# Multiplying all columns of a scale vector before the first q matmul, and loading them ahead of the q weights

## The chip, the cores and the metric

One core of a Trainium2 chip. The metric is device time in microseconds (us) of one execution. PE is TensorE, PEld its weight load, DVE VectorE, ACT ScalarE, SP the engine whose queue issues the loads, POOL GpSimd. PSUM is the memory that matmuls write to; copying a result out of it is called its evacuation.

## The reference, cut to what matters

A transformer block with adaptive layer norm: 2048 tokens, width 1024, linear attention, then a gated feed-forward layer. What matters here is the first modulation:

```
mod = silu(c) @ w_mod                       # six vectors of 1024: sa, ca, ga, sb, cb, gb
h = layernorm(x) * (1 + ca) + sa            # ca: the first scale vector, sa: the first shift vector
q, k, v = split(h @ wqkv)
```

## The kernel before: the parts that matter

All loads go through one queue, in program order. `WCA` holds the part of `w_mod` for `ca`, in two halves of 512 columns (1 MB each). `WQK[:, i]` holds the q weights for input slice i (128 of the 1024 inputs; 0.25 MB each).

```
for st in range(4): load x tile st          # 4 x 0.25 MB
ca_load(0)                                  # columns 0..3 (blocks of 128) of the scale vector
wq_load(0, 2)                               # q weights, slices 0 and 1
ca_load(1)                                  # columns 4..7
wq_load(2, 2); wq_load(4, 2); sa_load(1) ...
```

A column block of the scale vector is eight matmuls with one output column each, accumulated in PSUM. DVE then adds 1:

```
def mod_sc(w, c0, ms):
    for m in ms:
        for kt in range(NDT):               # 8
            P.pe("matmul", out=PS[:, 0, c0 + m:c0 + m + 1], lhsT=w[:, kt, m * 128:(m + 1) * 128],
                 rhs=SILUC[:, kt:kt + 1], start=mod_first[0], stop=(kt == NDT - 1), ...)
def fin_ca(m, n):
    P.dve("tensor_scalar", out=MODCOL[:, 0, m:m + n], in0=PS[:, 0, 8 + m:8 + m + n], scalar1=1.0, ...)
```

The front and the first q phase, in program order (each engine works in order; cut):

```
warm(13)                                    # fillers: 128x512 matmuls on zeros
... DVE, ACT: layer norm of tiles 0..3
tile_transposes(0); warm(5); tile_transposes(1)
ln1_xn(2); ln1_xn(3)                        # DVE: normalize tiles 2 and 3
mod_sc(WCA, 8, range(2)); fin_ca(0, 2)      # columns 0,1
tile_transposes(2, 3)
h0_first(0), h0_first(1)                    # DVE: slice of h = (1 + ca) * transposed tiles
# q phase
for nt in range(4): q_part(nt, qb[nt], (0,))
mod_sc(WCA, 8, range(2, 4)); fin_ca(2, 2)   # columns 2,3
h0_first(2), h0_first(3)
... 10 more q matmuls on slices 0 and 1
mod_sc(WCA, 8, range(4, 8)); fin_ca(4, 4)   # columns 4..7
... 14 q matmuls on slices 2 and 3, 8 on slice 4 and 5
mod_sc(WSA, 0, range(6, 8))                 # the first one-column matmuls on the SHIFT columns: "the marker"
```

The start of that last line is called the marker below. Between the first q matmul on slice 2 and the marker there are always the same 22 q matmuls, in every version, so the marker tells when the part that the change touches was over.

## Time and profile before

| | |
|---|---|
| time, median of 3 | 831.89 us (831.71 to 832.13) |
| span of the profiled execution | 829.7 us |
| PE busy | 99% of it |
| marker | 20.76 us |

The page, its part on busy time and its part on the chain that ended last:

```profile
PE 819.3 (99%) x4005; PEld 378.6 (46%) x4083; DVE 311.0 (37%) x665; ACT 196.3 (24%) x335; POOL 40.7 (5%) x58
...
PE 96%; DVE 2%; issue 1%; DMA 0%; ACT 0%; POOL 0%; DVEq 0%; ACTq 0%
```

PE bounds the kernel, and it runs nearly without a gap.

The front on PE's weight loads, from the timeline of the kernel before (start us, length us, group, count, and in brackets the idle time before it and what ended it):

```profile
7.20 0.45 PEld L176 LDWEIGHTS ps<-ident,xres 128*128 128x128 bf16 x8 [0.39 <-DVE xres L176]
7.60 0.80 PEld L176 LDWEIGHTS ps<-e,ident 128*128 128x128 bf16 x5
9.27 0.45 PEld L176 LDWEIGHTS ps<-ident,xres 128*128 128x128 bf16 x8 [0.87 <-ACT xres L176]
9.96 0.46 PEld L176 LDWEIGHTS ps<-siluc,wca 128*128 128x128 bf16 x16 [0.23 <-DMA wca<-in_w_mod_dram]
10.35 0.10 PEld L176 LDWEIGHTS ps<-ident,xres 128*128 128x128 bf16 x1
10.70 0.84 PEld L176 LDWEIGHTS ps<-ident,xres 128*128 128x128 bf16 x15 [0.26 <-DVE xres L176]
11.76 0.56 PEld L176 LDWEIGHTS ps<-ht,wqk 128*128 128x128 bf16 x4 [0.22 <-issue]
12.44 0.67 PEld L176 LDWEIGHTS ps<-siluc,wca 128*128 128x128 bf16 x16
13.03 1.84 PEld L176 LDWEIGHTS ps<-ht,wqk 128*128 128x128 bf16 x10
15.00 1.06 PEld L176 LDWEIGHTS ps<-siluc,wca 128*128 128x128 bf16 x32
15.99 0.55 PEld L176 LDWEIGHTS ps<-ht,wqk 128*128 128x128 bf16 x4
```

Transposes read `xres`, fillers `e`, scale columns `siluc,wca`, q matmuls `ht,wqk`. The first q weights are loaded at 11.76 us. Before 11.76 there are holes. Just one is ended by a load of the scale columns (0.23 us, until 9.96). After it there is none.

What held the first q matmul back is shown by the chain of waits:

```profile
9.29 0.79 POOL rstd L176
10.08 0.03 issue
10.10 0.56 DVE xres L176
10.66 0.05 issue
10.71 1.01 PE ps L176 x15
```

It is the normalization of tile 3 (`xres`, 10.10 to 10.66) and then its transposes.

The loads of the two scale halves, issue and time to landing, from the DMA view of the two stretches in which they are issued (columns: count, KB, us to landing; issued at 2.65 and 4.00 us):

```profile
wca<-in_w_mod_dram SPq DMA_DIRECT2D x1, 1024.0 KB, 7.3
...
wca<-in_w_mod_dram SPq DMA_DIRECT2D x1, 1024.0 KB, 10.3
```

So the first half lands at 2.65 + 7.3 = 9.95 us and the second at 4.00 + 10.3 = 14.3 us. PE uses the second at 15.00: its load is hidden behind q matmuls.

### The profile page before, as it was taken

To read this page: it belongs to the slowest core of one execution; us is meant where nothing else is said; L and a number is where in the kernel's file an instruction comes from. 1 tells how busy PE (TensorE), PEld (TensorE's weight loads), DVE (VectorE), ACT (ScalarE), POOL (GpSimd) and SP (SyncE) were. 2 spreads that over 40 slices of the span, in tenths; PEclk is the share of its full clock that TensorE was granted. 3 is DMA by queue.
4 is the path that set the end of the run, shared out by engine and by line. 5 is a ranking of instruction groups with operands and counts; after the bars stand their busy time and mean duration, and the time that the engine had idled before them with its cause. 6 is when DMAs were issued, how large, how long until landed. Compare 5 with 4: busy or idle time off the path is not lost.

```text
span 829.7 us, 9938 instructions
## 1 busy us (share of the span) xinstructions
PE 819.3 (99%) x4005; PEld 378.6 (46%) x4083; DVE 311.0 (37%) x665; ACT 196.3 (24%) x335; POOL 40.7 (5%) x58
## 2 busy tenths in 40 slices
PE   8999999999999999999999999999999999999998
PEld 4544444454444444444444444444444444444444
DVE  5797986756955521121221112122111111111111
ACT  3757641323232111111111101111110111111011
POOL 1010000000130000030000003000000300000000
DMA  9969656928297995700455571045557004553000
GB/s 321 289 151 231 148 156 172 202 102 304 56 248 233 283 264 153 197 25 13 123 152 152 152 188 34 13 125 152 156 150 192 26 16 125 152 154 88 0 26 26
DMA packets 199247, 119.29 MB, mean 144 GB/s; under 512 B 57881, under 2 KB 182945, under 8 KB 199201
## 3 DMA queue, kind: packets, MB, share of 16 engines
q1 hardware_dynamic: 199184, 118.65, 52.7%
q8 instruction: 32, 0.52, 0.3%
q14 instruction: 15, 0.11, 0.0%
q10 hardware_dynamic: 16, 0.00, 0.0%
HBM read 100.67 MB, written 4.33 MB: 127 GB/s over the span
## 4 chain that ended last, share of the span: by engine, by line
PE 96%; DVE 2%; issue 1%; DMA 0%; ACT 0%; POOL 0%; DVEq 0%; ACTq 0%
PE ps L176 96%; DVE acc L176 1%; DVE stats L176 0%; DMA xres<-in_A_x_dram 0%; DVE pkt L176 0%; DVE e L176 0%; DVE xres L176 0%; DVE pqt L176 0%; POOL rstd L176 0%; DVE mv L176 0%; ACT mw L176 0%; ACT e L176 0%; DVE ve L176 0%; DVE ut L176 0%; DVE ht L176 0%
## 5 line engine op out<-in xcount | busy, mean ns | idle before, releaser
L176 PE MATMUL ps<-h2t,guu 128*128 128x512 bf16 x879 | 210.3, 379 | 0.9
L176 PE MATMUL ps<-h2t,gug 128*128 128x512 bf16 x878 | 209.9, 379 | 0.9
L176 DVE TENSOR_TENSOR at<-sg,ps 128x512 bf16<-128x512 bf16 x112 | 77.0, 687 | 284.8 <-PE ps L176 274.9
L176 ACT ACTIVATE sg<-ps 128x512 bf16<-128x512 f32 x112 | 66.9, 597 | 309.7 <-PE ps L176 298.3
L176 PEld LDWEIGHTS ps<-h2t,guu 128*128 128x128 bf16 x896 | 87.7, 98 | 105.7
L176 PEld LDWEIGHTS ps<-h2t,gug 128*128 128x128 bf16 x896 | 87.6, 98 | 105.5
L176 PE MATMUL ps<-wd_a,at 128*128 128x512 bf16 (+2 forms) x518 | 113.0, 372 | 0.5
L176 PE MATMUL ps<-ht,wqk 128*128 128x512 bf16 x499 | 110.5, 379 | 1.0 <-DVE ht L176 0.3
L176 PE MATMUL ps<-wd_b,at 128*128 128x512 bf16 (+2 forms) x388 | 85.3, 372 | 0.4
L176 PEld LDWEIGHTS ps<-wd_a,at 128*128 128x128 bf16 x528 | 51.0, 98 | 59.8
L176 DVE TENSOR_TENSOR ut<-att,gb_b 128x512 bf16<-128x512 bf16 (+1 forms) x32 | 14.1, 440 | 167.0 <-ACT att L176 167.0
L176 PEld LDWEIGHTS ps<-ht,wqk 128*128 128x128 bf16 x512 | 49.4, 98 | 58.6 <-issue 0.2
L176 ACT ACTIVATE att<-ps 128x512 bf16<-128x512 f32 (+1 forms) x32 | 17.4, 591 | 182.1 <-PE ps L176 182.1
L176 PEld LDWEIGHTS ps<-wd_b,at 128*128 128x128 bf16 x396 | 38.3, 98 | 44.7
L176 PE MATMUL ps<-pk,xres 128*128 128x512 bf16 x250 | 56.0, 379 | 0.4 <-issue 0.2
L176 PE MATMUL ps<-mw,pqt 128*128 128x512 bf16 x250 | 55.7, 379 | 0.3
L176 POOL TENSOR_SCALAR h2t<-h2t,modcol 128x512 bf16<-128x512 bf16 x32 | 26.4, 843 | 383.2 <-DMA h2t<-xn 383.2
L176 ACT ACTIVATE e<-ps 128x512 bf16<-128x512 f32 x56 | 33.2, 604 | 31.7 <-PE ps L176 20.7
L176 PEld LDWEIGHTS ps<-mw,pqt 128*128 128x128 bf16 x256 | 24.9, 98 | 29.9 <-DVE xres L176 0.4
L176 PEld LDWEIGHTS ps<-pk,xres 128*128 128x128 bf16 x256 | 24.8, 98 | 30.1 <-DVE g L176 0.4
L176 ACT ACTIVATE junk<-xres 128x1024 bf16<-128x1024 bf16 x24 | 25.4, 1058 | 35.5 <-DVE xres L176 35.2
L176 DVE SCALAR_TENSOR_TENSOR xres<-ps,xres 128x512 bf16<-128x512 f32 x32 | 21.5, 688 | 12.2 <-PE ps L176 12.0
(102 smaller groups left out, 339.4 us busy)
## 6 DMA issues: line engine op xcount, KB each, us to landing
gug<-in_B_w_gate_dram SPq DMA_DIRECT2D x56, 512.0 KB, 4.0
guu<-in_B_w_up_dram SPq DMA_DIRECT2D x56, 512.0 KB, 5.3
xres<-in_A_x_dram SPq DMA_DIRECT2D x20, 256.0 KB, 7.8
rb<-recip_den SPq DMA_DIRECT2D x8, 512.0 KB, 11.5
stgx<-in_w_mod_dram SPq DMA_DIRECT2D x2, 2048.0 KB, 8.0
wd_a<-in_B_w_down_dram SPq DMA_DIRECT2D x4, 1024.0 KB, 7.9
out_dram<-xres SPq DMA_DIRECT2D x31, 128.0 KB, 1.7
xres<-in_A_x_dram SPq DMA_DIRECT2D x3, 1024.0 KB, 14.1
```

What stands on the lines that cost most here:

```text
L176: return getattr(e, method)(**kw)
```

## The change

Its intent: no one-column matmuls between the first q matmuls. All columns are to be multiplied where PE has holes and runs fillers anyway, and both scale halves are loaded ahead of the q weights so that they come in time. The change also splits the load of q slices 0 and 1 in two and moves two slices of h from DVE to ACT.

```
         ca_load(0)
-        wq_load(0, 2)
         ca_load(1)
+        wq_load(0)
+        wq_load(1)
         wq_load(2, 2)
...
         tile_transposes(0)
-        warm(5, bank=3)
+        warm(3, bank=3)
+        mod_sc(WCA, 8, range(4))
         s3_[0]()
         ln1_xn_act(1)
         tile_transposes(1)
...
         ln1_xn(2)
+        fin_ca(0, 4)
         ln1_xn(3)
-        mod_sc(WCA, 8, range(2))
-        fin_ca(0, 2)
-        tile_transposes(2, 3)
+        tile_transposes(2)
+        warm(2, bank=3)
+        tile_transposes(3)
+        mod_sc(WCA, 8, range(4, 8))
         h0_first(0, "dve")
         h0_first(1, "dve")
+        h0_first(2, "act")
+        h0_first(3, "act")
+        fin_ca(4, 4)
...
-            for nt in range(4):
-                q_part(nt, qb[nt], (0,))
-            mod_sc(WCA, 8, range(2, 4))
-            fin_ca(2, 2)
-            for dt in (2, 3):
-                h0_first(dt, "dve")
-            for nts, dts in (((4, 5), (0,)), (range(6), (1,)), ((6,), (0, 1))):
+            for nts, dts in ((range(4), (0,)), (range(4), (1,)), ((6, 4, 5), (0, 1))):
                 for nt in nts:
                     q_part(nt, qb[nt], dts)
-            mod_sc(WCA, 8, range(4, 8))
-            fin_ca(4, 4)
```

## The prediction

> **What bounds the kernel now.** The page gives PE 99% busy of 829.7 us; the chain that ended last is 96% PE. From the first q matmul (about 11.8 us; timeline) PE runs almost without a gap, so a microsecond won or lost before the second half of the first q phase passes through to the end.
>
> The first 30 us are also DMA-bound: the slices show 350 to 380 GB/s. Landings (DMA view, issue plus time to landing): first half of the scale columns 2.65 + 7.3 = 9.95 us (PE's weight load waits for it, 9.73 to 9.96); q weights 0,1 at 11.3; second half 4.00 + 10.3 = 14.3; q weights 2,3 at 15.7. About 1.5 us lie between the queue having moved a transfer's bytes and its landing. The Trainium skill, "DMA: Bandwidth & Descriptors", section "Anatomy of one DMA", puts a fixed part of about 2 us down mostly to the write receipt; the trace agrees in kind, with 1.5.
>
> **What the change does.** It takes 48 one-column matmuls (16 at 12.65, 32 at 15.21 us; 0.41 + 0.85 us of PE) out of the q phase and puts all 64 before it, where PE has holes (0.38 us at 8.9, 0.23 at 9.73, about 0.3 at 10.4) and fillers (0.22 us each, now 3 + 2 for 5). Bytes are unchanged; the second scale half overtakes q weights 0 and 1.
>
> **What it costs**, estimated from these durations, PE being in order:
> - The first 32 one-column matmuls wait for the landing, still 9.95 us (nothing ahead of it changes), and end at 10.8; PE idles from 8.5. The transposes of tile 1, ready at 9.2, now stand behind them: to 11.25.
> - DVE's normalization of tile 3, now behind the first evacuation, ends near 11.65, not 10.65. Transposes of 2, two fillers, transposes of 3: to about 12.5.
> - The second half lands 0.5 MB earlier: about 12.85. Its 32 matmuls run to 13.7. q weight 0 lands about 13.5, q weight 1 about 14.25: just in time.
> - First q matmul at 13.7 instead of 11.8. The 14 q matmuls on slices 0 and 1, now uninterrupted, take 14 x 0.221 = 3.1 us: to 16.8. Before, those on slices 2,3 begin at 16.23.
>
> So this part gets 1.3 us shorter but begins 1.9 us later: a loss of about 0.55 us. PE waits for no later load, so nothing gives it back. The intent would pay only if the scale columns landed by about 8.5 and 11.8 us; and the q matmuls that hid the second half's load now stand behind it.
>
> **Prediction.** 831.89 + 0.55 = 832.4 us, range 831.8 to 833.2. Faster by over 2%: 0.005; within 2%: 0.99; slower by over 2%: 0.005.
>
> **What would show it.** PE waits about 1.4 us for the first scale load, until 9.95, and again for the second, until 12.85; first q matmul near 13.7, none of one column among the first 14; slices 2,3 begin near 16.8; everything later shifted by the same 0.5 us.
>
> **What would make it wrong.** (1) The second half landing well before 12.8: then equal or slightly faster. (2) The clock gate: the Trainium skill, "TensorE: Matmul & The Clock Gate", section "What's actually happening", says that an idle window of about 3.4 us brings the half clock back. Here matmuls start 0.43 us apart until about 5.8 us, then 0.22. The changed front has holes of 1.4 and 0.4 us among small matmuls; should it fall back, the first q matmuls would be 0.43 us apart and the loss 1 to 3 us. I give this 10%. (3) Slack later, in the stretch at 82 to 95 us where DVE leads the chain, that swallows the shift: then no change.

## More of the kernel before

Every execution has a mean granted TensorE clock in its record (1.0 is full).

The program issues one weight load for each matmul, so 4005 matmul records against 4083 weight loads say that 78 matmul records are missing: where an exact start matters, read the weight loads.

## The result, and the profile after

| | before | after |
|---|---|---|
| median of 6 (same rounds) | 831.80 us | 832.05 us |
| lowest to highest | 831.57 to 832.81 | 831.74 to 832.58 |
| span of the profiled execution | 829.7 | 830.1 |
| first q weight load | 11.76 | 13.39 |
| marker | 20.76 | 21.18 |

Ratio 1.0002, 95% interval 0.9989 to 1.0014: the same. (A ratio is the mean time of one kernel's fast runs over that of the other's in the same rounds, so it is not quite the ratio of the medians.) All executions were fast ones, none of them over 1.5% above the fastest of its kernel.

The chain of waits of the changed kernel, in place of the one through tile 3:

```profile
2.65 0.43 SPq L176
3.08 0.04 issue
3.12 9.43 DMA wca<-in_w_mod_dram
12.55 0.05 issue
12.60 87.41 PE ps L176 x531
```

The first q matmul now hangs on the load of the second scale half, from its issue at 3.12 to its landing at 12.55 us. The front on PE's weight loads:

```profile
7.77 0.69 PEld L176 LDWEIGHTS ps<-ident,xres 128*128 128x128 bf16 x8 [0.28 <-issue]
8.43 0.37 PEld L176 LDWEIGHTS ps<-e,ident 128*128 128x128 bf16 x3
9.62 0.86 PEld L176 LDWEIGHTS ps<-siluc,wca 128*128 128x128 bf16 x32 [0.83 <-DMA wca<-in_w_mod_dram]
10.41 0.90 PEld L176 LDWEIGHTS ps<-ident,xres 128*128 128x128 bf16 x16
11.27 0.15 PEld L176 LDWEIGHTS ps<-e,ident 128*128 128x128 bf16 x2
11.54 0.65 PEld L176 LDWEIGHTS ps<-ident,xres 128*128 128x128 bf16 x8
12.60 0.87 PEld L176 LDWEIGHTS ps<-siluc,wca 128*128 128x128 bf16 x32 [0.41 <-DMA wca<-in_w_mod_dram]
13.39 2.92 PEld L176 LDWEIGHTS ps<-ht,wqk 128*128 128x128 bf16 x15
```

There are two waits for scale columns instead of one, and the first q weights are loaded at 13.39, 1.63 us later. In return the q matmuls run uninterrupted: those on slice 2 begin at about 13.39 + 14 x 0.2156 = 16.41 us, against 15.99 before (0.2156 us is the pace of the 36 q matmuls from 13.42 to the marker at 21.18). The first 14 q matmuls and what stood among them took 4.23 us before and 3.02 after. So 1.63 us later and 1.21 us shorter: 0.42 us lost between these two executions, and the marker and the span show the same 0.4. How much of it is the change comes under e1 and e2.

The time to landing of the two halves, issued at 2.65 and 3.12 us:

```profile
wca<-in_w_mod_dram SPq DMA_DIRECT2D x1, 1024.0 KB, 6.9
...
wca<-in_w_mod_dram SPq DMA_DIRECT2D x1, 1024.0 KB, 9.4
```

In this execution the first half landed at 9.55 us, 0.4 earlier than in the profile of before, although nothing ahead of it in the queue had changed. This spread between executions is the noise that the experiments had to cope with.

### The profile page after: what moved, and what is told of

The parts are those of the page before. It is cut to its first block, busy times and chain, and to the rows that moved or that the text cites. A ratio compares the mean times of both kernels' runs of the same rounds, so it can differ in the third digit from the quotient of the medians.

```text
span 830.1 us, 10017 instructions
## 1 busy us (share of the span) xinstructions
PE 824.2 (99%) x4083; PEld 379.0 (46%) x4083; DVE 310.3 (37%) x662; ACT 197.4 (24%) x337; POOL 40.5 (5%) x58
## 4 chain that ended last, share of the span: by engine, by line
PE 98%; DMA 1%; SPq 0%; ACT 0%; DVE 0%; issue 0%
PE ps L176 98%; DMA wca<-in_w_mod_dram 1%; SPq L176 0%; ACT mw L176 0%; DVE ut L176 0%; DVE xres L176 0%
```

## The experiments

Theory A: PE works in order, so one-column matmuls that stand ahead of the q matmuls hand them the landing time of the scale columns; the gain (48 one-column matmuls out of the q phase) is real but smaller than the delay. Rivals: B, there is no loss, the profiles differ only by when the clock opened, and the order is of little weight; C, a later stretch swallows the shift. D, formed on the way: holes in the front can let the clock gate fall back.

A summary first. "First landing" is the first scale half by the DMA view, "first q" the first q weight load; all from the profiles.

| kernel | first landing | first q | marker | span | span less marker |
|---|---|---|---|---|---|
| before | 9.95 | 11.76 | 20.76 | 829.7 | 808.9 |
| e1 before again | 10.05 | 12.02 | 21.02 | 829.9 | 808.9 |
| after | 9.55 | 13.39 | 21.18 | 830.1 | 808.9 |
| e2 after again | 9.65 | 13.50 | 21.29 | 830.4 | 809.1 |
| e3 new order, old loads | 10.85 | 16.14 | 23.93 | 832.8 | 808.9 |
| e4 old order, new loads | 10.25 | 13.96 | 22.95 | 831.8 | 808.9 |
| e5 no scale wait, new loads | 9.44 | 13.17 | 20.95 | 830.1 | 809.2 |
| e6 no scale wait, old loads | 10.15 | 12.24 | 20.70 | 829.6 | 808.9 |
| e7 columns 2,3 early | 10.25 | 12.20 | 20.85 | 829.7 | 808.9 |
| e8 after + 20 fillers | 10.45 | 18.45 | 26.44 | 835.3 | 808.9 |
| e9 first half early | 10.45 | 13.24 | 21.88 | 830.7 | 808.8 |
| e10 after less 2 fillers | 9.95 | 13.76 | 21.55 | 830.4 | 808.9 |
| e11 as e5 | 9.95 | 13.62 | 21.40 | 830.2 | 808.8 |
| e12 e5 + 3 fillers | 9.45 | 13.12 | 20.91 | 829.7 | 808.8 |

The last column is flat within 0.4 us while the marker moves by 5.7: what happens before the marker passes through to the end in full. So a shift of the marker is a shift of the end. Each marker is of one execution, though, and shares its spread; what helps is that the trace shows from which event that execution's marker followed.

### e1, e2: both kernels again

No edit.

> The kernel before, unchanged, against itself: the noise. Ratio 1.000 within 0.1%. Its profile: the first one-column matmul on the shift columns (the marker, 20.76 us in the profile of before) again at 20.5 to 21.0 us. Theory A (the landing of the scale columns decides) expects the marker to be steady even if the full clock comes 1 us later or earlier; theory B (the 0.4 us between the two profiles is only where the clock gate opened, 5.8 us against 8.0 us) expects a late opening here to move the marker to about 21.2 us.

> The changed kernel, unchanged. Theory A: marker at 21.0 to 21.4 us whenever the clock opens, because PE waits for the second scale half until 12.5 to 12.9 us; time 0.2 to 0.6 us above before. Theory B: with an early opening (before 6.5 us) the marker falls to 20.8 us and the time is that of before.

e1: median 832.28 against 831.72 of the same kernel in the same rounds, ratio 1.0007 (0.9994 to 1.0021). e2: 832.31, ratio 1.0007 (0.9994 to 1.0019). The kernel before differs from itself by as much as the changed kernel differs from it: timing in one set of rounds can't resolve the effect. (e2 against e1 is 0.03 us by the medians.) All executions of before (40) and of after (11), on several chips, have means of 831.91 and 832.18, 0.27 us apart; given what e1 shows, this is support and no more.

The markers are 21.02 for e1 and 21.29 for e2. In these two profiles the clock opened at the same time (fillers 0.43 us apart until about 7 us), so that it can't make the difference between them: 0.27 us of loss, with the first q 1.48 us later. Of the 0.42 us in the first pair, part may thus have been the execution and not the change. (The profile's granted clock reads 1.00 in that stretch too, so the opening is read from the spacing.) For B, e1 lies between the two values (21.2 was B's for a late opening), but its chain of waits shows another cause: in e1 the first x tile landed at 3.71 us and not at 3.46, and that 0.25 us runs through DVE and POOL to tile 3 and on to q, with no filler in the chain. For the changed kernel the opening before 6.5 us that B's number supposed did not come about; it came a microsecond earlier than in the first profile, and the marker was no lower (21.29 against 21.18).

The chains of the two (from e1, then from e2) hang on different events, tile 3 and the second scale half:

```profile
0.79 2.92 DMA xres<-in_A_x_dram
9.54 0.79 POOL rstd L176
10.36 0.56 DVE xres L176
...
3.12 9.54 DMA wca<-in_w_mod_dram
```

In the changed front the marker follows the landing of the second half: 8.63, 8.62, 8.63 and 8.64 us after it in after, e2, e10 and e8 (less the 4.31 us of its fillers, below), while that landing moves from 12.55 to 13.49 us. In the kernel before the marker follows tile 3: POOL's `rstd` of tile 3, a step that the change does not touch, starts at 9.29 and 9.54 us in the two profiles, and the marker comes 11.47 and 11.48 us later. So one can estimate where the old order would have put the marker in the executions of the changed front. Their `rstd` starts at 9.66 (after), 9.24 (e2), 9.78 (e10) and 9.67 (e8); plus 11.475 that is 21.13, 20.71, 21.25 and 21.14, and the markers are 21.18, 21.29, 21.55 and 22.13 (e8 less its fillers). By this estimate the change lost about 0.05, 0.6, 0.3 and 1.0 us, on average 0.5. It is a race between two events, and most of the 0.42 us between the first two profiles came from x, which was 0.37 us later at tile 3 in the second.

Over all 14 profiles the first landing has a mean of 9.84 us with the new loads (8 profiles, 9.44 to 10.45) and of 10.28 with the old ones (6, 9.95 to 10.85). Whether what stands behind a transfer in the queue hastens it, or this is chance, the runs don't settle.

### e3, e4: each half of the change alone

e3 has the changed matmul order with the old loads, e4 the old matmul order with the new loads:

```
e3 (from after)              e4 (from before)
 ca_load(0)                   ca_load(0)
+wq_load(0, 2)               -wq_load(0, 2)
 ca_load(1)                   ca_load(1)
-wq_load(0)                  +wq_load(0)
-wq_load(1)                  +wq_load(1)
```

> The changed matmul order with the old load order (q weights 0,1 ahead of the second scale half). Theory A: second half lands at 14.0 to 14.3 us, first q matmul at about 15.1, marker at about 23.0 us, time about 2.3 us above before (834.1). Theory B (order of little weight): marker within 0.5 us of 21.2 and time within 0.5 us of before.

> The old matmul order with the new load order. Theory A: q weight 0 lands at about 13.2 us and the first q matmul waits for it, so all after it, with its 1.3 us of one-column matmuls still inside, begins 1.4 us later: marker at about 22.3 us, time about 1.6 us above before (833.4). So either half of the change alone would cost 1.6 to 2.3 us and both together only 0.4. Theory B: marker within 0.5 us of 20.8, time within 0.5 us of before.

e3: 834.05 us, ratio 1.0029 (1.0016 to 1.0041). e4: 833.59 us, ratio 1.0030 (1.0017 to 1.0043). Both times are within 0.2 us of theory A's; the markers, 23.93 and 22.95, are 0.9 and 0.65 later than it said, in executions whose first landing was 0.9 and 0.3 later than in the profile of before. B falls: each half alone has its interval clear of 1. In e4 the first q matmul waits for its own weights, which stand behind both scale halves (matmuls of e4 around it, timeline):

```profile
10.71 1.37 PE L176 MATMUL ps<-ident,xres 128*128 128x128 bf16 x16
13.97 1.04 PE L176 MATMUL ps<-ht,wqk 128*128 128x512 bf16 x4 [1.89 <-DMA wqk<-in_A_wqkv_dram]
```

In e3 the second half landed at 15.3 us and held everything. Either half alone costs about 2 us. Together they cost 0.3 to 0.4 by the markers of the two pairs, 0.5 by the estimate under e2, because the matmul order makes use of what the load order hurries and does without what it delays.

Two of five executions of e4 took 835.33 and 835.65 us, the others 833.3 to 833.6; those two have a mean granted clock of 0.998, the others of 1.0. The profiled execution of e3 had 0.998 too, and shows where (stretches of e3: length, busy time of each engine, then the granted clock, DMA share, GB/s):

```profile
8.00:10.88 2.88, 1.35 (x13) 0.65 (x11) 1.82 (x7) 1.30 (x3) 1.33 (x2) 1.00 1.07 382
10.88:13.40 2.52, 2.52 (x49) 2.52 (x50) 0.62 (x2) 0.00 (x0) 0.00 (x0) 0.61 1.09 360
13.40:15.30 1.90, 1.74 (x12) 1.01 (x10) 0.54 (x2) 0.35 (x1) 0.00 (x0) 0.62 1.06 381
15.30:17.00 1.70, 1.65 (x36) 1.20 (x37) 0.93 (x3) 1.70 (x3) 0.00 (x0) 1.00 1.08 359
```

After a stretch in which PE waited for the late first half, the granted clock averaged 0.61 and 0.62 over the next 4.4 us, a loss of about 1.7 us of full clock (0.39 x 2.52 + 0.38 x 1.90), most of it hidden here behind the wait for the second half. Cut finer, the same view gives 1.00 up to about 11.4 us, 0.50 from 11.45 to 14.80 and 1.00 from 14.90: one stretch of 3.4 us at half clock, begun half a microsecond after PE had work again. Half of 3.4 us in a span of 832.8 makes a mean of 0.998, two such stretches 0.996. Of the ten executions with a lower clock in all these runs nine have 0.998 and one has 0.996, so each may have had one such stretch, or two; that is an estimate. That is the risk the prediction gave 10%. The changed kernel itself did not meet it: all 11 of its executions have 1.0, as have all 34 of before in the rounds of these experiments.

### e5, e6: the scale columns taken out of the front

The early one-column matmuls read the identity matrix, which is always there, in place of the scale columns; loads and instruction counts stay. The result is wrong (the comparison with the reference did not notice, the scale being small beside 1). e5 has the new loads, e6 the old ones.

```
-    lhsT=w[:, kt, m * 128:(m + 1) * 128]
+    lhsT=IDENT[:] if w is WCA else w[:, kt, m * 128:(m + 1) * 128]
```

> The changed kernel, its 64 early one-column matmuls reading the identity in place of the scale columns (wrong result on purpose; same loads, same instructions). If the landing of the scale columns alone holds the first q matmul back (theory A), it starts near 12 us as soon as that wait is gone, and the marker falls to about 20.4. If q weight 0, now behind both scale halves in the queue, holds it nearly as long (theory A2: the load order has two gates close together), the first q matmul waits for it until about 13.2 to 13.4 us and the marker moves only by 0.1 to 0.3, to about 21.0 us.

> The same with the old load order (wrong result on purpose). Theories A and A2: q weight 0 is there by 11.4 us, the first q matmul starts at about 12.0, the 14 on slices 0 and 1 end at about 15.1, and then q weights 2,3 hold PE until they land at about 15.7: marker at about 20.4 us, some 0.3 to 0.5 us before that of the kernel before, and no more, as the loads set a floor. A theory in which the order of matmuls costs by itself (theory B) expects a marker no better than 20.8 us.

A2 (two gates close together) is right in both. e5 (matmuls, timeline) waits for its q weights where the changed kernel waited for scale columns:

```profile
11.59 0.94 PE L176 MATMUL ps<-siluc,ident 128*128 128x1 bf16 x32
13.17 7.94 PE L176 MATMUL ps<-ht,wqk 128*128 128x512 bf16 x36 [0.64 <-DMA wqk<-in_A_wqkv_dram]
```

Its marker is 20.95, 0.23 us below the changed kernel's: even with the scale columns free of charge, the new load order has a second gate, the q weights of slice 0, that opens only 0.2 us before the one it replaces. e6 starts q at 12.24 and then stops at the next gate:

```profile
12.27 3.18 PE L176 MATMUL ps<-ht,wqk 128*128 128x512 bf16 x14
15.94 4.92 PE L176 MATMUL ps<-ht,wqk 128*128 128x512 bf16 x22 [0.49 <-DMA wqk<-in_A_wqkv_dram]
```

The q weights of slices 2 and 3 were not there until 15.9. The marker, 20.70, is 0.06 and 0.32 us below the two of before (expected: 0.3 to 0.5). In this execution the loads let no more be gained by hiding all 64 one-column matmuls.

Times: e5 median 832.95, ratio 1.0017 (1.0003 to 1.0031); e6 831.72, ratio 1.0005 (0.9992 to 1.0017). (Executions with a lower clock are in the ratios.) Three executions of e5, with clocks of 0.996 to 0.998, took 834.0 to 835.8; the three at 1.0 took 831.8 to 831.9. One of e6 at 0.998 took 834.8. Neither profiled execution was such a one.

### e7: just the columns that are there

The kernel before, with columns 2,3 (already landed with 0,1) multiplied ahead; nothing else moved. Correct.

```
-        mod_sc(WCA, 8, range(2))
-        fin_ca(0, 2)
+        mod_sc(WCA, 8, range(4))
+        fin_ca(0, 4)
         tile_transposes(2, 3)
...
-            mod_sc(WCA, 8, range(2, 4))
-            fin_ca(2, 2)
```

> The kernel before with only columns 2,3 of the scale (which are in the first half, landed at about 10 us) multiplied ahead, with 0,1, where PE waits for tile 3; loads, transposes and the second half as before. Correct result. Theory A: 16 one-column matmuls (0.4 us) leave the q phase and mostly fill a hole: first q matmul at most 0.1 us later, marker 0.25 to 0.35 us earlier than before's 20.8 to 21.0, so 20.4 to 20.7; time 0.3 us below before, which timing can't resolve. Theory B: marker at 20.8 or later.

Marker 20.85: the stated 20.4 to 20.7 was missed, in an execution whose tile 3 was late. Its `rstd` starts at 9.65 us, for which the old order would have put the marker at 21.13 by the estimate under e2, so 0.28 us were gained, as expected. Four executions took 831.33 to 831.58; the fifth, at a clock of 0.998, took 833.13. Median 831.45 against 831.78, ratio 0.9999 (0.9987 to 1.0011). So the gain of some 0.3 us rests on that estimate from one profile; timing does not show it, and one dip of the clock (the slow execution is 1.7 us above its kernel's median) takes it back.

### e8: a known delay in front

Twenty fillers more just ahead of the first q matmul of the changed kernel.

```
         mod_sc(WCA, 8, range(4, 8))
+        warm(20, bank=3)
         h0_first(0, "dve")
```

> The changed kernel with 20 filler matmuls more just ahead of the first q matmul (20 x 0.2213 = 4.4 us). If a shift of the first q matmul passes through to the end (theory A): marker 25.6 to 25.7 us and time 4.4 us above the changed kernel's (836.5). If later slack swallows shifts (theory C): time less than 4 us above it while the marker moves by 4.4.

The fillers took 18.67 - 14.36 = 4.31 us (start of the first q matmul less start of the fillers). The marker was at 26.44 and not at 25.7, as the first half landed at 10.45, 0.8 to 0.9 later than in the profiles of after; from the landing it is 15.99, and less the 4.31 it is 11.68 (after: 11.63, 11.64). Span less marker is 808.9 as everywhere: C falls. Time 836.9, 4.6 to 4.9 above the medians of after; in the profiled execution (837.03) the late landing accounts for the rest over 4.3, and the others' landings are not known.

### e9: only the first half ahead of tile 1

Old loads, second half at its old place; the first half's matmuls stand where the change puts them.

```
(from before)
-        warm(5, bank=3)
+        warm(3, bank=3)
+        mod_sc(WCA, 8, range(4))
...
         ln1_xn(2)
+        fin_ca(0, 4)
         ln1_xn(3)
-        mod_sc(WCA, 8, range(2))
-        fin_ca(0, 2)
...
-            mod_sc(WCA, 8, range(2, 4))
-            fin_ca(2, 2)
```

> Old loads, second half at its old place; only the first half's 32 one-column matmuls stand where the change puts them, ahead of tile 1's transposes. If the first gate (waiting for the first half with tile 1 ready behind) were what costs, the marker would be at 21.2 us or later. Theory A, which puts the loss on the second gate, expects first landing + 10.8 to 10.9 us, so 20.6 to 21.0 for a landing at 9.8 to 10.1: level with before, 0.2 to 0.4 us ahead of the changed kernel.

Theory A as I had put it here fell: the marker is 21.88, 11.43 after the first landing and not 10.8 to 10.9. In the profiled execution the first gate alone costs too. (By time it does not show: median 831.96 against 831.87, ratio 1.0001, 0.9987 to 1.0014, and the profiled execution is the slowest of four.) The prediction had named the reason, and I had left it out of this expectation: DVE also works in order, and the normalization of tile 3 stands behind the evacuation of the scale columns (DVE in e9, timeline):

```profile
9.63 0.54 DVE L176 TENSOR_SCALAR xres<-xres,mv,rstd 128x1024 bf16<-128x1024 bf16 x1
11.51 0.16 DVE L176 TENSOR_SCALAR modcol<-ps 128x4 f32<-128x4 f32 x1 [1.34 <-PE ps L176]
11.59 0.54 DVE L176 TENSOR_SCALAR xres<-xres,mv,rstd 128x1024 bf16<-128x1024 bf16 x1
```

DVE sits idle for 1.34 us with tile 3 still to do, and PE then waits for tile 3 at 12.18. So the first q weight load comes 3.45 us after the start of tile 3's `rstd` (9.79), against 2.47 and 2.48 in before: 1.0 us later, for 0.4 us of matmuls taken out. The marker is 0.6 us later than the estimate under e2 has for the old order (21.27). In the changed kernel the second gate comes last, and it alone decides.

### e10: the changed kernel without its two late fillers

```
         tile_transposes(2)
-        warm(2, bank=3)
         tile_transposes(3)
```

> The changed kernel without its two fillers between the transposes of tiles 2 and 3. Theory A alone: PE reaches the second half 0.4 us earlier, waits 0.4 us longer, marker unchanged (21.2 to 21.3 at a first landing of 9.6 to 9.7), time that of the changed kernel. Theory D (the clock gate needs the fillers): in some executions the granted clock falls below 1, and some of the times are 833 us and more.

The wait for the second half is 0.63 us instead of 0.2, the marker is 11.60 us after the first landing as in the changed kernel, the time 832.04, ratio 1.0000 (0.9986 to 1.0013), all five clocks 1.0. The two fillers neither cost nor, in five executions, protect anything: D's expectation for this kernel was not met.

### e11, e12: the slow executions of e5

e11 is e5. e12 adds three fillers in the hole ahead of the first q matmul:

```
         mod_sc(WCA, 8, range(4, 8))
+        warm(3, bank=3)
         h0_first(0, "dve")
```

> The kernel whose early one-column matmuls wait for no load (new loads) once more: three of its six executions took 834 to 836 us and three 831.8 to 831.9. Theory D (clock gate): if this one is a slow one, its profile shows a granted clock clearly below 1 in some stretch between 9 and 20 us and q matmuls 0.43 us apart, worth the 2 to 4 us; if it is a fast one, no such stretch. Rival (E): the slow executions lose the time elsewhere, at a clock of 1.

> The same kernel with three fillers in the hole just ahead of the first q matmul, which waited there 0.6 us for its weights. Theory D: no execution above 833 us, median 831.8 to 832.1, marker 20.9 to 21.1. Rival E: slow executions of 834 us and more as before.

e11 fell on a fast execution (831.99 us, clock 1.0; a single run, so its state is unknown), and says nothing on the slow ones. It does bear on e5: its marker, 21.40, lies above the changed kernel's 21.18, as its first half landed at 9.95. With the new loads both gates wait for the same queue, so here the first landing is the right start: 11.51, 11.45 and 11.46 us to the marker in e5, e11 and e12, against 11.60 to 11.68 with the changed front. The two gates are 0.1 to 0.2 us apart. e12: 831.52 to 834.54, median 832.98, ratio 1.0011 (0.9998 to 1.0024). The fillers did not cure it; the slowest again has 0.998, while 832.98 and 833.2 stand at 1.0. Over all kernels, each of the ten executions with a recorded clock under 1.0 is slower than every execution of its kernel at 1.0; that they lose time by a dip of the clock is well supported, and e3 shows one such dip. What sets it off in e4 to e7 and e12, where in the program it falls there, and why the changed kernel is spared, stays open: no execution of those with a dip fell on a profile.

## Why the prediction was right

The stated range, 831.8 to 833.2, holds the time of the kernel before as well, so the measured time would also have fitted a change without effect. What the runs test is the mechanism.

- **What bounds.** Right: a shift ahead of the marker passes through to the end one for one (span less marker flat; e8).
- **First gate.** Right in kind: PE and DVE stand behind the first half's landing. PE's wait was to be 1.4 us and was 0.83 (its weight loads), as the clock opened later and the fillers took longer, and as the half landed earlier; in e2 it was 1.40. In e9's profile this alone delays q by 1.0 us.
- **Second gate.** Right: predicted landing 12.85, measured 12.55 and 12.67 (e2), but the first half, too, landed 0.4 earlier than in the profile of before. The distance between the two landings was to be 2.9 us and was 3.0.
- **q begins later, and is shorter.** Predicted 1.9 later and 1.3 shorter; measured 1.63 and 1.21 in the first pair, 1.48 later in the matched one. The sum was to be a loss of 0.55 us. The markers say 0.42 and 0.27, the medians 0.25, and the estimate under e2 has 0.05 to 1.0, on average 0.5: right in sign, and about right in size, but the size of one execution depends on which of two events comes late in it. The prediction took both as fixed.
- **The mis-sized term.** "Those on slices 2,3 begin at 16.23" was the first *recorded* matmul; by its weight loads, which are complete, it was 15.99. "14 x 0.221" used a pace from a stretch with missing records; it is 0.2156. By luck the two errors nearly cancel (16.8 less 16.23 was predicted, 16.41 less 15.99 measured). The Trainium skill ("TensorE: Matmul & The Clock Gate", "Wait — 56ns, not 53.3ns?") has 215.7 ns for 512 columns and a floor of about 25 ns for small matmuls, which agrees with 215.6 ns here, and with 32 one-column matmuls in 0.82 us (12.60 to 13.42), 25.6 ns each. Beyond that, the landing of the loads differs by up to 1.4 us between executions, and a prediction from one profile takes it for fixed.
- **The clock gate.** The Trainium skill ("TensorE: Matmul & The Clock Gate", "What's actually happening") was used for a 10% risk. It did not happen in 11 executions of the changed kernel, and did in its relatives (0.50 for 3.4 us in e3).
- **Landing after the bytes.** The Trainium skill ("DMA: Bandwidth & Descriptors", "Anatomy of one DMA") gives about 2 us of fixed cost, but for transfers issued from GpSimd, and these loads go through SP's queue, so the prediction could not rest on it. By the cumulative bytes of the queue in the trace of before, the landings came 1.5 to 1.6 us after the last byte was due, in that of after about 1.0. The predicted gain in landing of the second half rested on counting bytes ahead of it, and that held.

Where did the expected gain go? The 1.2 us are there. They are paid for by a queue that holds 1 MB per scale half: in the old order the second half came in while q matmuls that did not need it were running; in the new one they wait for it.

## What to carry to other kernels

Filling a hole with work is free only if the work's inputs are there when the hole is: compare landing times with the hole's start before moving it, and look at every engine that works in order, since the evacuation drags its own queue along. When two orders (loads and matmuls) fit each other, test each alone as well; either half of this change costs about 2 us, the whole about 0.3 to 0.5. And where an effect is smaller than the spread of timing, find a marker in the trace behind which nothing changes, and measure it from the event that it hangs on; that event need not be the same in the two kernels (here tile 3 before, the second scale half after).

## What the Trainium skill lacked or had wrong

- "TensorE: Matmul & The Clock Gate", section "What's actually happening", speaks of an idle window of about 3.4 us before the half clock comes back, and "Why this matters for your kernels" of gaps over about 3 us. In e3 the clock fell to 0.50 at about 11.4 us, although PE had been busy for 1.88 of the 3.41 us before and its longest single wait in them was 2.0 us (by the waits of its weight loads). A whole idle window was not needed there. The length of the hole does not decide it alone either: one of 2.3 us in e9's profile brought no fall. What does, no run shows.
- No page that I know of gives the spread of a landing between executions: the same transfer, fifth in the same queue behind the same bytes, landed between 9.4 and 10.9 us in 14 profiles.
